# Two VectorE operations of a gate polynomial issued right behind the squares in every batch of a fused attention and expert kernel

## The chip, the cores and the metric

The kernel runs on one core of a Trainium2 chip. The metric is the device time of one launch in microseconds, as the median of several runs. Five engines work side by side, each through its own queue of instructions: TensorE (PE; its weight loads are shown as PEld), VectorE (DVE), ScalarE (ACT), GpSimd (POOL) and SyncE (SP), which here only issues DMAs.

## The reference

Attention with mixed heads, then a dense layer with an odd gate, then slots of experts. The part that the change touches is the second:

```python
x = attn_out.transpose(0, 2, 1, 3).reshape(B * S, H * D)   # 1792 tokens x 768
h = x @ w_in                     # w_in: 768 x 2048
g = h - np.tanh(h)
x = g @ w_out                    # w_out: 2048 x 768
# then: logits = x @ phi; softmax over tokens and over slots; experts; combine
```

## The kernel before, in words

The program is one sequence of Python calls under a manual schedule: each engine executes its instructions in the order in which the calls issue them, and semaphores are put in between by the framework.

After attention, stage 1 computes h and g in transposed form. The 1792 tokens are cut into four passes of 512, 512, 512 and 256 tokens, the 2048 features into 16 blocks of 128. A batch is one block of one pass, so there are 64 batches, numbered t. The function `step(t)` issues TensorE's product of batch t (18 matrix multiplies into one PSUM bank, tile `hp`, L830) and, through hooks between its six groups of three, everything else: the gate of batch t - 1, the transposition of the gate of batch t - 2 (`turn_g`, L900 on TensorE, copied out on ScalarE, L903), and side work.

The gate computes g = h - tanh(h), and for small h, where that difference would lose its digits, a polynomial in h squared. `gate_act` issues on ScalarE the square of h into the PSUM tile `sq` (L849), the square of the shifted square into `qd` (L850), tanh into `g` (L855) and a mask that is positive where h is small (`mk`, L856). Between the second square and tanh it calls `beside`, which splits the weights of batch t + 1 into a high and a low part, on ScalarE and GpSimd (L777 and L778 in pass 0, nothing in passes 1 and 2, halves at L786 and L787 towards pass 3). `gate_poly` issues two VectorE operations on `qd` and `sq` (L860, L861). `gate_first` subtracts tanh from h (L868), and `gate_last` finishes the polynomial into `hp` (L873) and copies it over `g` where the mask is set (L874). `gate_first` is issued at hook 1 and `gate_last` at hook 4. In pass 3 (`t >= LAST`, LAST = 48) `gate_act` itself calls `gate_poly`.

The side work of pass 0 (steps 3 to 16) prepares w_out @ phi: `turn_w` transposes three blocks of a weight at a time on TensorE (L953) into the PSUM bank that `turn_bank` hands out in turn (two banks, one used by `turn_g` in between), and a copy takes them out, on VectorE for the first half of a row of blocks (L959), on ScalarE for the second (L957). The first `turn_w` of a step is at hook 1 ahead of `gate_first`, the second at hook 3. The steps 5, 9, 13 and 16 also fold the transposed weights (L965, L973, L975). Steps 2 to 12 convert the last weights from 64-bit floats, on ScalarE (L50), VectorE (L54 to L66, five operations) and GpSimd (L71). In steps 8 to 13 the activations of the next pass are split, on ScalarE (L813) and GpSimd (L814). In steps 18 and 34 hook 1 begins with `mix_t` and `slot_exp`, whose first VectorE operation is a reduction (L1011).

Of the kernel before, what the change touches and what calls it, by code (L numbers as in the profile page):

```python
# [636 lines left out]
def moe_and_slots(tc, ident, xd, wi, wo, wo4, wis, consts, w1, w2, out, box):  # L637
# [27 lines left out]
    LAST = NST - NF  # L665
# [12 lines left out]
    def bank(tag, shape, name):  # L678
        return bank_pool[tag].tile(shape, FP32, tag=tag, name=name)
# [156 lines left out]
    def temps_of(t):  # L836
        n = PASS[t // NF]
        if t < 2:
            part = [quad[:, i * n:(i + 1) * n] for i in range(4)]
            return part[0], part[1], part[2], part[3] if t else mem["g0"]  # L840
        i = (t - LAST) % 2 * n if t >= LAST else 0
        return mem["sq"][t], mem["qd"][:, i:i + n], mem["mk"][:, :n], g_of(t)

    def gate_act(t, beside=None):
        hp = hps[t]
        if t > 1:
            mem["sq"] = {t: bank(f"q{t % 2}", [128, PASS[t // NF]], "sq")}
        sq, qd, mk, g = temps_of(t)
        nc.scalar.activation(out=sq, in_=hp, func=ACTF.Square)  # L849
        nc.scalar.activation(out=qd, in_=sq, func=ACTF.Square, bias=tshift)  # L850
        if t >= LAST:
            gate_poly(t)
        if beside:
            beside()
        nc.scalar.activation(out=g, in_=hp, func=ACTF.Tanh)  # L855
        nc.scalar.activation(out=mk, in_=sq, func=ACTF.Relu, bias=tlimit, scale=-1.0)  # L856

    def gate_poly(t):
        sq, qd, mk, g = temps_of(t)
        nc.vector.scalar_tensor_tensor(out=qd, in0=qd, scalar=TG_E, in1=sq, op0=ALU.add, op1=ALU.mult)  # L860
        nc.vector.scalar_tensor_tensor(out=qd, in0=sq, scalar=-TG_A, in1=qd, op0=ALU.add, op1=ALU.mult)  # L861

    def gate_first(t):
        hp = hps[t]
        sq, qd, mk, g = temps_of(t)
        if t < LAST:
            gate_poly(t)
        nc.vector.tensor_tensor(out=g, in0=hp, in1=g, op=ALU.subtract)  # L868

# [214 lines left out]
    def step(t):  # L1084
# [14 lines left out]
        if t > 2:  # L1099
            split_half(t + 1, 0)  # L1100
            gate_act(t - 1, lambda: split_half(t + 1, 1) if t >= NF else split_w(t + 1, nc.gpsimd))
        else:
            split_w(t + 1, nc.gpsimd)
# [4 lines left out]
        if t > 2:  # L1108
            on(1, gate_first, t - 1)
# [75 lines left out]
    load_w(4)  # L1185
    mem["g0"] = keep.tile([128, TM], FP32, tag="lp", name="g0")
    gate_act(0)
    yield
    split_w(2, nc.vector)
    product(1, {})  # L1190
    load_w(5)
    gate_first(0)
    gate_last(0)
    yield
    gate_act(1)
    while not box.get("go"):
        yield
    gate_first(1)
    gate_last(1)
    acc_stack = ExitStack()  # L1200
# [28 lines left out]
    t = NST  # L1229
# [300 lines left out]
```

## Time and profile before

| | us |
|---|---|
| median of three runs | 899.65 (894.24 to 904.73) |
| the profiled execution | 899.93 |
| its span | 898.2 |
| TensorE busy | 823.1 (92%) |
| ScalarE busy | 573.5 (64%) |
| VectorE busy | 556.1 (62%) |
| GpSimd busy | 257.0 (29%) |

The profile is of one execution. Stage 1 lies between 446 us and 790 us of its span: pass 0 up to about 556, passes 1 and 2 up to about 730, pass 3 up to about 787. In rows of the timeline the columns are start, length, engine, line, operation, output and inputs by name, shapes, and, in brackets, how long the engine was idle before and which instruction released it. The engines start an operation a little before the one ahead of it has ended, so the spacing of starts is the measure of a chain.

### The profile page before, as it was taken

Reading aid. Unit: us, or ns where it says so; the run is one execution under the profiler, and the core shown is the slowest. Engines: PE = TensorE matmul, PEld = TensorE weight load, DVE = VectorE, ACT = ScalarE, POOL = GpSimd, SP = SyncE. Lnnn points to the kernel's source line nnn. Section 1 sums busy time; section 2 is a strip of 40 time slices with the busy share of each in tenths; the row PEclk is TensorE's granted clock in tenths of the full one; section 3 lists DMA queues with packets and bytes.
Section 4 is the critical chain, followed back from the end, with each engine's and each line's share of the span. In section 5 each row is a group of like instructions: output and inputs, shape, how many; then the busy total and the mean of one; then the engine's idle time right before and its main releaser. Section 6 shows DMA issues by size and latency. Waiting matters only on the chain.

```text
span 898.2 us, 28617 instructions
## 1 busy us (share of the span) xinstructions
PE 823.1 (92%) x11760; PEld 581.5 (65%) x11760; DVE 556.1 (62%) x1181; ACT 573.5 (64%) x1351; POOL 257.0 (29%) x438
## 2 busy tenths in 40 slices
PE   8878989889987999999999899999999989999995
PEld 6456666666655666666776676767767767864542
DVE  4456857677766777777467886557776767720103
ACT  4766877778867788878656775647555656621013
POOL 6343434444434334434212561000000035500000
PEclk9989999999999999999999999999999999997998
DMA  6988889887989888774869976688745445899997
GB/s 133 227 215 231 220 215 235 238 226 215 226 217 236 233 208 243 238 216 154 261 216 374 346 243 215 258 306 325 284 162 176 158 141 193 284 380 426 416 372 267
DMA packets 145622, 222.95 MB, mean 248 GB/s; under 512 B 60820, under 2 KB 127444, under 8 KB 142036
## 3 DMA queue, kind: packets, MB, share of 16 engines
q1 hardware_dynamic: 142144, 208.26, 74.4%
q10 hardware_dynamic: 3348, 12.87, 3.6%
q8 instruction: 93, 1.52, 0.7%
q14 instruction: 37, 0.30, 0.1%
HBM read 146.39 MB, written 36.18 MB: 203 GB/s over the span
## 4 chain that ended last, share of the span: by engine, by line
PE 57%; ACT 13%; DMA 12%; DVE 12%; issue 4%; POOL 1%; SPq 0%; ACTq 0%; POOLq 0%; DVEq 0%
PE hp L830 21%; DMA D<-S 9%; PE pm L321 5%; ACT e L333 5%; PE vx L403 5%; PE sc L287 4%; PE tm L364 4%; DVE mx L325 3%; PE h L1314 3%; ACT S L295 2%; PE so L1355 2%; PE gt L900 2%; PE tz L1334 2%; ACT aT L378 2%; PE lgp L984 2%
## 5 line engine op out<-in xcount | busy, mean ns | idle before, releaser
L333 ACT ACTIVATE e<-pm,mx 128x448 f32<-128x448 f32 x184 | 115.1, 632 | 81.8 <-DVE mx L325 78.5
L830 PE MATMUL hp<-xa,rg 128*128 128x512 f32 x576 | 153.1, 405 | 0.6 <-ACT xa L813 0.4
L325 DVE TENSOR_REDUCE mx<-pm 128x1 f32<-128x448 f32 x184 | 106.1, 618 | 76.2 <-PE pm L321 76.0
L364 PEld LDWEIGHTS tm<-wk,e 64*56 64x56 f32 x5888 | 108.5, 130 | 57.0 <-issue 30.7
L321 PE MATMUL pm<-D,wpre 64*64 64x448 f32 (+2 forms) x736 | 113.0, 566 | 19.1 <-DMA D<-S 16.8
L364 PE MATMUL tm<-wk,e 64*56 64x60 f32 x5888 | 117.5, 218 | 10.1 <-issue 5.3
L830 PEld LDWEIGHTS hp<-xa,rg 128*128 128x128 f32 x576 | 102.2, 188 | 30.0 <-issue 10.5
L295 ACT ACTIVATE S<-sc 120x448 f32<-120x448 f32 (+1 forms) x186 | 91.4, 552 | 13.8 <-DMA kn<-in_k_dram 5.8
L287 PE MATMUL sc<-khi,qT 64*120 64x448 f32 (+1 forms) x384 | 84.0, 395 | 9.2 <-DVE xs L413 6.5
L787 POOL TENSOR_TENSOR rg<-rg 128x384 fp32r<-128x384 f32 x32 | 32.0, 1012 | 207.0 <-DVE rg L784 195.2
L339 POOL TENSOR_SCALAR rv<-ss 128x2 f32<-128x2 f32 x92 | 24.5, 267 | 229.1 <-ACT e L333 191.0
L350 POOL TENSOR_SCALAR wk<-wpost,rv 128x60 f32<-128x60 f32 x184 | 85.2, 494 | 16.2 <-DVE rv L343 14.5
L403 PE MATMUL vx<-aT,vn 128*64 128x120 f32 (+1 forms) x1536 | 85.3, 263 | 3.7 <-issue 3.2
L403 PEld LDWEIGHTS vx<-aT,vn 128*64 128x64 f32 x1536 | 74.8, 138 | 10.5 <-issue 5.6
L860 DVE SCALAR_TENSOR_TENSOR qd<-qd,sq 128x512 f32<-128x512 f32 (+1 forms) x62 | 38.3, 617 | 64.1 <-ACT mk L856 57.6
L849 ACT ACTIVATE sq<-hp 128x512 f32<-128x512 f32 (+1 forms) x62 | 32.8, 529 | 70.4 <-PE hp L830 70.2
L378 ACT ACTIVATE aT<-tm 128x480 f32<-128x480 f32 x144 | 75.8, 593 | 0.4 <-PE tm L364 0.4
L830 PE MATMUL hp<-xb,rg 128*128 128x512 f32 x288 | 74.7, 404 | 0.0
L287 PEld LDWEIGHTS sc<-khi,qT 64*120 64x120 f32 (+1 forms) x384 | 46.3, 176 | 26.1 <-PE tm L364 7.9
L830 PEld LDWEIGHTS hp<-xb,rg 128*128 128x128 f32 x288 | 52.0, 188 | 16.6 <-issue 6.3
L321 PEld LDWEIGHTS pm<-D,wpre 64*64 64x64 f32 (+2 forms) x736 | 24.8, 132 | 56.8 <-DMA D<-S 22.6
L71 POOL TENSOR_TENSOR fa<-fa,f 128x384 f32<-128x384 f32 x56 | 57.4, 1026 | 7.2 <-DVE rv L343 3.4
(194 smaller groups left out, 1407.9 us busy)
## 6 DMA issues: line engine op xcount, KB each, us to landing
ex<-in_moe_w_dram SPq DMA_DIRECT2D x25, 1536.0 KB
D<-S SPq DMA_DIRECT2D x144, 210.0 KB
rg<-wis SPq DMA_DIRECT2D x32, 768.0 KB
f<-in_moe_w_in_dram SPq DMA_DIRECT2D x32, 384.0 KB
wis<-rg ACTq DMA_DIRECT2D x16, 768.0 KB
rg<-wi SPq DMA_DIRECT2D x26, 384.0 KB
f<-in_moe_w_out_dram SPq DMA_DIRECT2D x24, 384.0 KB
wi<-fa SPq DMA_DIRECT2D x32, 192.0 KB
```

What stands on the lines that cost most here:

```text
L71: eng.tensor_tensor(out=out, in0=bits(a), in1=bits(p), op=ALU.add)
L287: nc.tensor.matmul(xs[e][0][:ni], lhsT=qT[n][s, l, p, :ni], rhs=kt[s], start=(i == 0), stop=(i == 2))
L295: nc.scalar.activation(out=dst, in_=xs[e][0][:ni], func=ACTF.Copy)
L321: nc.tensor.matmul(xs[x][64 * i:64 * i + 64], lhsT=wpre[k0:k1], rhs=d[i][k0:k1], start=True, stop=True)
L325: nc.vector.tensor_reduce(out=mx[:, x:x + 1], in_=xs[x], op=ALU.max, axis=AX.X, negate=True)
L333: nc.scalar.activation(out=es[x], in_=xs[x], func=ACTF.Exp, bias=mx[:, x:x + 1], accum_out=ss[:, x:x + 1])
L350: nc.gpsimd.tensor_scalar(out=wk, in0=wpost, scalar1=rv[:, x:x + 1], scalar2=None, op0=ALU.mult)
L364: nc.tensor.matmul(xs[i][64 * z:64 * z + JH, x, c], lhsT=es[x][h, j:j + JH], rhs=wks[x][h], start=True, stop=True)
L378: nc.scalar.activation(out=out[:, :, c0:c0 + m].rearrange("p a (x i) -> p a x i", x=2), in_=x, func=ACTF.Copy)
L403: nc.tensor.matmul(x[64 * e:64 * e + 64, i, :ni], lhsT=nat_v[b, h // NP][:, h % NP, c, :], rhs=a[:, c, h, :ni], start=(c == 0), stop=(c == ...
L830: nc.tensor.matmul(hp, lhsT=r32(w[:, m, hl, cs]), rhs=r32(x_of(b, c, l)), start=(c == 0 and i == 0), stop=(c == KD - 1 and i == 2))
L860: nc.vector.scalar_tensor_tensor(out=qd, in0=qd, scalar=TG_E, in1=sq, op0=ALU.add, op1=ALU.mult)
```

## The change

The two VectorE operations of `gate_poly` are issued by `gate_act` itself, right behind ScalarE's two squares, in the batches 2 to 47 as well as in pass 3; until now they were issued by `gate_first` in these. Batches 0 and 1 keep the old place. Nothing else is changed.

```diff
@@ gate_act
         nc.scalar.activation(out=sq, in_=hp, func=ACTF.Square)
         nc.scalar.activation(out=qd, in_=sq, func=ACTF.Square, bias=tshift)
-        if t >= LAST:
+        if t > 1:
             gate_poly(t)
         if beside:
             beside()
@@ gate_first
         sq, qd, mk, g = temps_of(t)
-        if t < LAST:
+        if t < 2:
             gate_poly(t)
         nc.vector.tensor_tensor(out=g, in0=hp, in1=g, op=ALU.subtract)
```

## Rows read from the trace of the kernel before

**Rows 1.** Busy time by stretch: PE, PEld, DVE, ACT, POOL, clock, DMA, GB/s

```profile
465.00:556.00 91.00, 85.45 (x470) 62.34 (x469) 70.08 (x125) 61.90 (x111) 38.86 (x27) 1.00 0.86 306
556.00:730.00 174.00, 173.44 (x884) 125.99 (x883) 116.92 (x196) 100.79 (x185) 2.03 (x2) 1.00 0.62 225
```

**Rows 2.** Waits of PE and of PEld from 465 to 730: total us, times, longest

```profile
PE wt L953 <- DVE ex L959: 3.2, 4, 1.1
...
PEld gt L900 <- issue: 3.5, 11, 0.5
```

**Rows 3.** Timeline of pass 1: the gate of one batch

```profile
600.62 0.58 ACT L849 ACTIVATE sq<-hp 128x512 f32<-128x512 f32 x1 [2.19 <-PE hp L830]
...
601.24 0.69 ACT L850 ACTIVATE qd<-sq,tshift 128x512 f32<-128x512 f32 x1
...
603.02 0.69 DVE L860 SCALAR_TENSOR_TENSOR qd<-qd,sq 128x512 f32<-128x512 f32 x1 [2.41 <-ACT mk L856]
603.74 0.69 DVE L861 SCALAR_TENSOR_TENSOR qd<-sq,qd 128x512 f32<-128x512 f32 x1
604.35 0.68 DVE L868 TENSOR_TENSOR g<-hp,g 128x512 f32<-128x512 f32 x1
...
605.67 0.75 DVE L874 COPY_PREDICATED g<-mk,hp 128x512 f32<-128x512 int32 x1
...
606.53 0.42 PEld L900 LDWEIGHTS gt<-ident,g 128*128 128x128 f32 x4 [0.36 <-issue]
```

**Rows 4.** Timeline of pass 3: squares, polynomial and mask of one batch

```profile
779.05 0.47 ACT L850 ACTIVATE qd<-sq,tshift 128x256 f32<-128x256 f32 x1
...
779.55 0.42 DVE L860 SCALAR_TENSOR_TENSOR qd<-qd,sq 128x256 f32<-128x256 f32 x1
...
780.01 0.43 DVE L861 SCALAR_TENSOR_TENSOR qd<-sq,qd 128x256 f32<-128x256 f32 x1
...
780.47 0.47 ACT L856 ACTIVATE mk<-sq,tlimit 128x256 f32<-128x256 f32 x1 [0.26 <-DVE qd L861]
```

**Rows 5.** Timeline of pass 0: steps 7 and 8, squares and second weight transposes

```profile
493.96 0.58 ACT L849 ACTIVATE sq<-hp 128x512 f32<-128x512 f32 x1 [1.16 <-PE hp L830]
...
496.61 0.49 PE L953 MATMUL wt<-ident,ex 128*128 128x128 f32 x3
...
499.21 0.58 ACT L849 ACTIVATE sq<-hp 128x512 f32<-128x512 f32 x1 [0.84 <-PE hp L830]
...
502.50 0.55 DVE L959 COPY ex<-wt 128x384 f32<-128x384 f32 x1
...
503.11 0.55 PE L953 MATMUL wt<-ident,ex 128*128 128x128 f32 x3 [1.10 <-DVE ex L959]
...
505.76 0.58 ACT L849 ACTIVATE sq<-hp 128x512 f32<-128x512 f32 x1 [0.62 <-PE hp L830]
```

**Rows 6.** L54 by line (ns min/median/max); timeline of one L54 beside GpSimd

```profile
L54 DVE TENSOR_SCALAR ex<-ex x8: 334/530/1440, 478.9 to 528.3; 128x384 f32<-128x384 f32 x8
...
521.30 1.29 POOL L814 TENSOR_TENSOR xb<-xb 128x512 fp32r<-128x512 f32 x1 [3.30 <-ACT xb L813]
521.37 1.44 DVE L54 TENSOR_SCALAR ex<-ex 128x384 f32<-128x384 f32 x1
```

**Rows 7.** Timeline of pass 0, step 15: mask, second weight transpose

```profile
551.21 0.69 ACT L856 ACTIVATE mk<-sq,tlimit 128x512 f32<-128x512 f32 x1
...
552.33 0.31 PEld L953 LDWEIGHTS wt<-ident,ex 128*128 128x128 f32 x3 [0.42 <-ACT ex L957]
```

**Rows 8.** Timeline at the entry into pass 3: gate transposes of batches 46 and 47

```profile
730.15 0.58 ACT L849 ACTIVATE sq<-hp 128x512 f32<-128x512 f32 x1 [1.28 <-PE hp L830]
...
731.93 0.63 PE L900 MATMUL gt<-ident,g 128*128 128x128 f32 x4 [1.10 <-ACT qd L850]
...
733.31 0.69 DVE L860 SCALAR_TENSOR_TENSOR qd<-qd,sq 128x512 f32<-128x512 f32 x1 [1.29 <-ACT mk L856]
...
736.84 0.63 PE L900 MATMUL gt<-ident,g 128*128 128x128 f32 x4 [2.15 <-DVE g L874]
```

## The prediction, made blind

> **What bounds the kernel now.** I first read the busy time of each engine over two stretches: the steps of stage 1 that also transpose and fold weights (465 to 556 us, pass 0) and the plain ones (556 to 730 us, passes 1 and 2) [rows 1]. The reader is to see that TensorE is busy for 173.44 of 174.00 us in the second and for 85.45 of 91.00 us in the first, at a granted clock of 1.00 in both. So nothing that VectorE does sooner can win more than 0.56 us plus what hides inside TensorE's rows in passes 1 and 2, or 5.55 us in pass 0. The change can cost any amount wherever TensorE waits for something that now comes later. The list of waits says where it waits today: above all, four times for VectorE's copy of a transposed weight, 3.2 us in all [rows 2].
>
> Then I read one batch of pass 1 in order of time [rows 3]. The squares start at 600.62, the second at 601.24 (0.69 long, so done at 601.93), but the polynomial starts only at 603.02, released by ScalarE's mask. It reads the same PSUM tile, sq, as the mask does. In pass 3, where the two operations already stand behind the squares, the order is the reverse [rows 4]: the polynomial starts at 779.55, 0.03 after the second square ends, and now the mask starts at 780.47, 0.03 after the polynomial ends, released by it. So whichever of the two readers of sq is issued first makes the other wait. The change doesn't take the wait away, it turns it round: the mask will wait for the polynomial in all 46 batches from 2 to 47.
>
> **What moves.** No instruction is added or removed, and the two operations issue no DMA. On VectorE they overtake the copy of a transposed weight (L959), where hook 1 begins with one, and in steps 18 and 34 the reduction of slot_exp; the SP and GpSimd queues are not overtaken, for the split of the weights puts work on ScalarE and GpSimd only. On ScalarE nothing is reordered, but the mask waits, and behind it stand the copies L903 and L957, the absolute value for the conversion, the activations split and the next squares. In steps 18 and 34 the reduction goes up to 1.33 later, but its result is transposed on TensorE only a step later, so I take 0. The store of split weights, a DMA that ScalarE's queue issues behind the mask in pass 0, is read again sixteen steps later: 0 as well.
>
> The new chain, from the spacing of starts in rows 3: polynomial at squares + 0.62 + 0.69 + 0.03 = 1.34 instead of 603.02 - 600.62 = 2.40; its second half 0.72 later, the next VectorE operation 0.61 after that, at 2.67. The second half ends at 2.75, so the mask goes to 2.79. The chain up to the predicated copy, which now ends at 605.67 + 0.75, 5.80 after the squares, gets 1.06 shorter, and more where a split copy stands between square and tanh.
>
> **Cost 1: the weight copy behind the polynomial (pass 0).** Steps 3 to 16 transpose weights. The PSUM banks of these transposes alternate, the gate's transpose taking the one in between, so the second weight transpose of a step needs the bank of the first to have been copied out. Where that copy is VectorE's (steps 3, 5 to 14 and 16, twelve of them) the polynomial is now ahead of it. In a step without a wait, TensorE begins the second weight transpose 496.61 - 493.96 = 2.65 after the squares, and the next squares come 499.21 - 496.61 = 2.60 later [rows 5]. With the change: copy at 2.67, transpose 503.11 - 502.50 = 0.61 later, at 3.28, and then 505.76 - 503.11 = 2.65 to the next squares. That is 3.28 + 2.65 - 5.25 = 0.68 us per step, all of it on TensorE. Steps 6, 10 and 14 follow a fold, whose last products and the logits stand on TensorE ahead of the product: squares and polynomial pass under them, so I take 0 (0.68 each without that cover). Steps 3, 5, 7, 13 and 16 pay in full: 5 x 0.68 = **3.4** (ends 0, if the polynomial slips ahead of the transpose unseen, and 5 x 1.33 = 6.7, if all of it shows).
>
> In steps 8, 9, 11 and 12 VectorE is behind with conversion work, and these are the waits that rows 2 count. Swapping two neighbours in a full queue delays the copy by the polynomial's 1.33 (0.72 + 0.61), but the chain behind it is shorter, and VectorE gets rid of its backlog sooner. If the copy then goes at the free pace, the four steps cost 4 x 0.68 - 3.2 = -0.5. What speaks against a full recovery is one row: a conversion operation that takes 334 ns at best took 1440 ns where it began 0.07 us after a GpSimd subtraction of 1.29 us had [rows 6]. With the conversion some 1.3 us earlier, it meets that subtraction more often. I take one such loss of 1.1 us among the four steps: -0.5 + 1.1 = **+0.6** (ends -0.5 and 4 x 1.33 = 5.3).
>
> **Cost 2: the mask behind the polynomial.** In steps 4 and 15 the first weight copy is ScalarE's, behind the mask, and TensorE already waits for it in step 15 [rows 7]. The mask there is 0.69 long, and with the polynomial right behind it, as in rows 3, it starts 2.40 - 0.69 - 0.03 = 1.68 after the squares. It will start at 2.79: 1.1 us. In step 4 a split copy stands between and hides most of this; I take 0.4. Sum **+1.5** (ends 0.4 and 2.2). In passes 1 and 2 the mask's 1.1 us falls into ScalarE's waits for the next product (2.19 us ahead of the squares in rows 3); if that cover were gone, each step could lose the rest, but 1.0 us of it is left.
>
> Pass 0 in sum: 3.4 + 0.6 + 1.5 = **+5.5 us**.
>
> **Gain 1: gate transposes (passes 1 and 2).** The predicated copy ended at 606.42, and TensorE's load for a gate transpose started at 606.53 after 0.36 us idle [rows 3]: the chain is a little late there. In the list of waits such idle times stand before eleven gate transposes, 3.5 us together [rows 2]; they are of the weight loads, so a part of each is hidden by the multiply in flight. A chain that is 1.06 shorter ends them: about 0.1 each, **-1.0** (ends 0 and -3.5).
>
> **Gain 2: entry into pass 3.** Batches of 256 tokens follow batches of 512, and the gates of batches 46 and 47 are late: TensorE waits 1.10 and 2.15 us at its gate transposes [rows 8]. The releaser named in one row is the next square; by the clock the predicated copy had just ended. The first chain is shortened by more than 1.10. For the second, the polynomial goes from 733.31 to 730.15 + 1.34 = 731.49, so its end comes 1.82 sooner; together the two transposes can come no sooner than that: **-1.8** (ends 0, if a later load takes it back, and -3.25).
>
> **Sum.** 5.5 - 1.0 - 1.8 = +2.7 us. The profiled execution took 899.93 us (span 898.2 and 1.7 around it) and the median is 899.65; the sum is made on the former and added to the latter: **902.3 us**. Three runs of one kernel already lie between 894.24 and 904.73, so 1% (9 us) is about what a measurement can tell from no change.
>
> **Rivals.** *Slower: GpSimd holds VectorE up.* If the conversion operations, earlier by about the polynomial, meet a GpSimd subtraction in all eight converting batches, each loses 1440 - 334 = 1.1 us [rows 6], which the copy behind them hands to TensorE: 8 x 1.1 = 8.8 in place of 0.6, a sum of 3.4 + 1.5 + 8.8 - 2.8 = +10.9, 910.5 us. It decides where the conversion ends later than 1.34 us after the squares. For it: VectorE is already full there. Against: the shortest of the eight took 334 ns and the median one 530, so today most of them pass with little. The Trainium skill (SBUF — State Buffer, "Who interferes with whom") states this as a rule: VectorE in a two-port mode and GpSimd exclude each other for the length of an instruction, and whoever issues first goes first; rows 6 agree. Chance 0.14.
>
> *Faster: the copies are hidden.* VectorE reaches the polynomial before TensorE's first weight transpose is done and the copy keeps its time; only the mask's 1.5 is left, and both gains come whole: 1.5 - 1.0 - 3.25 = -2.8, 896.9 us. Against it: the copy would have to start at 2.04 for a transpose at 2.65, and the polynomial isn't through until 2.67. Chance 0.2.
>
> *It doesn't do what it says.* If the polynomial still waited for ScalarE's newest instruction, nothing would move: 899.7 us. Rows 4 speak against it. Chance 0.05.
>
> **How the numbers follow.** The forecast has 0.58, and 0.03 is left for what I don't see. The range goes from 895 (the hidden copies, less a part of the spread of runs) to 910.5 (GpSimd in the way). Faster by over 1% needs both gains whole and a lucky run: 0.05. Slower by over 1% is most of the slower rival's chance and a little of the forecast's: 0.13. Within 1%: 0.82.
>
> **What would show it.** In the changed profile the polynomial is released by the second square, 1.34 after the first, and the mask by the polynomial. TensorE's wait for the copy L959 grows from four times to nine or so and from 3.2 us to some 6; a step like the seventh takes 5.9 instead of 5.25 us; the stretch up to the first products of pass 1 is about 5.5 us longer, passes 1 and 2 about 1 us shorter, and the two waits of 3.25 us at the entry into pass 3 shrink to about 1.4. I am wrong if the steps with conversion take much more or less than 6.2 us each, if TensorE waits for ScalarE in passes 1 and 2, or if the last part, which is the same in both, changes by more than these sums.

## The result and the profile after

The changed kernel takes 908.74 us (median of 20 runs, 900.95 to 916.99) where the kernel before, run beside it, takes 901.07 (20 runs, 894.24 to 912.87). The ratio is 1.0088 with a 95% interval of 1.0067 to 1.0110: 7.7 us slower, 0.9%. The forecast was +2.7 us. The time lies inside the range and within 1%, but the cost is almost three times the forecast. Medians here are over all runs, ratios over those that are not in the slower state (over 1.5% above the fastest run of their kernel), so a ratio can differ from that of the two medians.

The profiled execution of after took 904.51 us (span 902.8). Its mean granted clock is 0.985, where the median of its 20 runs is 0.978 and the profiled execution of before has 0.978: it had less time at the lower clock than a usual run. The two stretches of rows 1, from the same step to the same step (columns as there):

```profile
468.00:566.10 98.10, 86.57 (x470) 61.94 (x469) 73.42 (x125) 62.54 (x111) 38.99 (x27) 1.00 0.81 284
566.10:740.70 174.60, 172.63 (x885) 126.69 (x883) 118.05 (x198) 103.13 (x185) 2.03 (x2) 1.00 0.62 224
```

The first is 98.10 - 91.00 = 7.10 us longer, yet TensorE is busy only 86.57 - 85.45 = 1.12 us more in it: what was added is waiting, at a clock of 1.00. The second is 0.60 longer, and that is one step of pass 0 (step 16) that still lies in it.

The chain of the gate turned round as expected. Timeline of after, the batch of rows 3:

```profile
612.53 0.58 ACT L849 ACTIVATE sq<-hp 128x512 f32<-128x512 f32 x1 [1.86 <-PE hp L830]
...
613.14 0.69 ACT L850 ACTIVATE qd<-sq,tshift 128x512 f32<-128x512 f32 x1
...
613.87 0.69 DVE L860 SCALAR_TENSOR_TENSOR qd<-qd,sq 128x512 f32<-128x512 f32 x1 [2.35 <-ACT qd L850]
...
615.31 0.69 ACT L856 ACTIVATE mk<-sq,tlimit 128x512 f32<-128x512 f32 x1 [0.99 <-DVE qd L861]
...
616.58 0.74 DVE L874 COPY_PREDICATED g<-mk,hp 128x512 f32<-128x512 int32 x1
```

The polynomial starts 613.87 - 612.53 = 1.34 after the squares, released by the second square, and the mask 2.78 after them, released by the polynomial after 0.99 us of standing still. The predicated copy ends 4.79 after the squares (5.80 before).

The waits of TensorE from 468 to 741 (total us, times, longest), against rows 2:

```profile
PE wt L953 <- DVE ex L959: 8.3, 8, 3.5
...
PE wt L953 <- ACT ex L957: 2.2, 2, 1.1
...
PE sp L1066 <- ACT quad L903: 1.5, 1, 1.5
```

The wait for VectorE's weight copy grew from four times and 3.2 us to eight times and 8.3 us, and one of the eight is 3.5 us. Nothing in the forecast is that long. The wait at L1066, in passes 1 and 2, is another that the forecast doesn't have (0.4 before). The eleven short idle times at the gate's transposes [rows 2] have left the list.

To see where each microsecond went I took the length of every step, from the start of its first square (L849) to the start of the next step's, and subtracted the kernel before's. A step from 3 to 16 repeats to 0.03 us when the kernel before is run again, so these differences say more than whole runs do, which scatter by 5 us and more. All that differs by over 0.1 us in steps 3 to 16 (the later rows are explained with the experiments):

| us more than before, by step | 3 | 4 | 5 | 6 | 7 | 8 | 9 | 11 | 12 | 13 | 15 | 16 | pass 0 |
|---|---|---|---|---|---|---|---|---|---|---|---|---|---|
| after | .24 | .37 | .67 | -.31 | .68 | 1.37 | 1.07 | .59 | .67 | .69 | 1.11 | .65 | +7.8 |
| after_again | .22 | .38 | .66 | -.31 | .68 | 1.35 | 2.66 | .58 | .67 | .69 | 1.09 | .65 | +9.3 |
| pass0_only | .23 | .38 | .66 | -.32 | .68 | .44 | 2.84 | .59 | .65 | .69 | 1.11 | .66 | +8.6 |
| store_front | .24 | .39 | .66 | -.32 | .68 | -.60 | .66 | .59 | .67 | .69 | 1.10 | .66 | +5.4 |
| mask_first | .81 | .01 | 1.24 | -.31 | 1.26 | -.04 | .67 | .58 | .66 | 1.26 | .00 | 1.23 | +7.4 |
| hook4 | -.02 | -.31 | .04 | -.33 | .02 | 1.36 | 1.83 | -.68 | .58 | .38 | .41 | -.02 | +3.3 |
| combined | .01 | -.31 | .06 | -.32 | .03 | -.67 | .68 | -.69 | .59 | .37 | -.18 | -.02 | -.4 |

In after_again, pass0_only and hook4 step 9 holds a stretch at the lower clock, worth some 1.6 us (below). After's other parts: steps 18 to 48 (passes 1 and 2) -0.07, the step at the entry into pass 3 (step 49) -1.82, the steps behind it -1.10. The sum of the steps is +4.79.

Most steps are what was worked out: 0.65 to 0.69 where 0.68 was expected. Steps 8 and 9 are not. Timeline of after, steps 7 to 9:

```profile
497.93 0.58 ACT L849 ACTIVATE sq<-hp 128x512 f32<-128x512 f32 x1 [1.16 <-PE hp L830]
...
500.71 0.69 ACT L856 ACTIVATE mk<-sq,tlimit 128x512 f32<-128x512 f32 x1 [0.26 <-DVE qd L861]
...
500.77 0.33 ACTq L791 DMA_DIRECT2D wis<-rg  x1
...
503.86 0.58 ACT L849 ACTIVATE sq<-hp 128x512 f32<-128x512 f32 x1 [1.15 <-PE hp L830]
...
506.64 0.69 ACT L856 ACTIVATE mk<-sq,tlimit 128x512 f32<-128x512 f32 x1 [0.26 <-DVE qd L861]
...
508.08 0.52 SPq L766 DMA_DIRECT2D rg<-wi  x1
...
509.58 0.33 ACTq L791 DMA_DIRECT2D wis<-rg  x1
...
509.96 0.60 ACT L903 ACTIVATE quad<-gt 128x512 f32<-128x512 f32 x1 [2.63 <-PE hp L830]
...
510.82 0.55 ACT L50 ACTIVATE ex<-ex 128x384 f32<-128x384 f32 x1
...
511.40 0.36 DVE L54 TENSOR_SCALAR ex<-ex 128x384 f32<-128x384 f32 x1 [2.28 <-ACT ex L50]
...
511.97 1.34 POOL L814 TENSOR_TENSOR xb<-xb 128x512 fp32r<-128x512 f32 x1 [3.80 <-ACT xb L813]
...
512.19 1.53 DVE L60 SCALAR_TENSOR_TENSOR ex<-ex 128x384 int32<-128x384 int32 x1
...
516.43 0.55 PE L953 MATMUL wt<-ident,ex 128*128 128x128 f32 x3 [3.45 <-DVE ex L959]
```

Follow ScalarE's queue. The store of split weights (L791) left at 500.77, 2.84 after the squares and 0.06 after the held mask began; in before it left at 494.64, 0.68 after the squares of the same step, while split, tanh and mask, which stand ahead of it in the program, had yet to begin. In the next step the mask starts at 506.64, and then ScalarE does nothing until its store gets away at 509.58: the 2.63 us of idle time at L903 (the releaser printed there, a product of TensorE, had long been done). Behind the store stand the copy L903 and the absolute value L50 of the weight conversion. VectorE idles 2.28 us for that value, the conversion's next operation L60 then falls on a GpSimd subtraction (1.53 us instead of 0.56), VectorE's weight copy comes late, and TensorE waits 3.45 us for it in step 9. Before, the store of step 8 left at 501.31, 2.10 after its squares; after, 5.72 after them.

### The profile page after: what moved, and what is told of

Same layout as the page of the kernel before. It is cut to its first block, busy times and chain, and to the rows that moved or that the text cites. A ratio compares the mean times of both kernels' runs of the same rounds, so it can differ in the third digit from the quotient of the medians.

```text
span 902.8 us, 28655 instructions
## 1 busy us (share of the span) xinstructions
PE 818.9 (91%) x11760; PEld 580.1 (64%) x11760; DVE 559.4 (62%) x1181; ACT 576.5 (64%) x1351; POOL 257.0 (28%) x438
## 3 DMA queue, kind: packets, MB, share of 16 engines
q8 instruction: 93, 1.52, 0.7%
## 4 chain that ended last, share of the span: by engine, by line
PE 55%; DMA 16%; ACT 12%; DVE 10%; issue 4%; POOL 1%; ACTq 0%; SPq 0%; POOLq 0%; DVEq 0%
PE hp L830 20%; DMA D<-S 7%; PE pm L321 6%; PE vx L403 5%; ACT e L333 5%; PE sc L287 5%; DMA ex<-in_moe_w_dram 5%; PE tm L364 4%; DVE mx L325 3%; ACT S L295 2%; PE gt L900 2%; DMA ex<-wo 2%; ACT aT L378 2%; PE sp L1066 1%; PE h L1314 1%
## 5 line engine op out<-in xcount | busy, mean ns | idle before, releaser
L364 PE MATMUL tm<-wk,e 64*56 64x60 f32 x5888 | 116.8, 217 | 14.9 <-issue 10.8
L856 ACT ACTIVATE mk<-sq,tlimit 128x512 f32<-128x512 f32 (+1 forms) x62 | 39.2, 632 | 43.3 <-DVE qd L861 43.3
L849 ACT ACTIVATE sq<-hp 128x512 f32<-128x512 f32 (+1 forms) x62 | 32.9, 530 | 45.5 <-PE hp L830 45.0
```

The lines of the kernel that those rows point to most:

```text
L364: nc.tensor.matmul(xs[i][64 * z:64 * z + JH, x, c], lhsT=es[x][h, j:j + JH], rhs=wks[x][h], start=True, stop=True)
```

## The experiments

Three theories were weighed. *Order*: VectorE's copy stands behind the polynomial on its own queue, and each step pays for that, whatever else goes on. *Store*: the store behind the held mask comes late, and what waits for it holds up step 8 or 9. *Full VectorE*: conversion and polynomial together are too much for VectorE in the full steps, or GpSimd holds it up; this is the slower rival grown large.

**Half of the change each.** In one kernel the early polynomial is kept in passes 1 and 2 alone, in another in pass 0 alone:

```
late_only:   gate_act: if t >= NF: gate_poly(t)                     gate_first: if t < NF: ...
pass0_only:  gate_act: if 1 < t < NF or t >= LAST: gate_poly(t)     gate_first: if t < 2 or NF <= t < LAST: ...
```

> Only the batches from 16 on (steps 17 to 48) have the polynomial early; the batches 2 to 15 are as before. If pass 0 pays and the later passes gain (my theory): ratio to before 0.997 to 0.999 (about -1.5 us for gate transposes, -1.8 at the entry into pass 3, +1.1 at the first sum over slots in step 22). If the mask's wait costs ScalarE something in every later step, the ratio is 1.003 or more. Pass 0 should take the same time as in the kernel before, within 0.5 us.

> Only the batches 2 to 15 (steps 3 to 16) have the polynomial early. If pass 0 pays: 6 to 8 us from the squares of step 3 to those of step 19 over the kernel before, and a ratio of 1.006 to 1.009. If the loss lies in the later passes, the ratio is below 1.003.

late_only: 894.95 against 902.22 us, ratio 0.9923 [0.9890, 0.9957], below the 0.997 to 0.999 that were expected. pass0_only: 909.02 against 902.22, ratio 1.0079 [1.0043, 1.0115]. So the loss is all in pass 0, and the rest of the change is a gain. By the steps, late_only has +0.16 up to the end of pass 0, the -1.82 of the entry and after's +1.1 in step 20 (the expectation calls it step 22); pass0_only has after's pass 0 but for steps 8 and 9, and none of these. In pass0_only ScalarE's idle time behind the store in step 8 is 1.68 us, and what it delays shows in step 9 (timeline of pass0_only):

```profile
510.91 0.33 ACTq L791 DMA_DIRECT2D wis<-rg  x1
...
511.29 0.60 ACT L903 ACTIVATE quad<-gt 128x512 f32<-128x512 f32 x1 [1.68 <-DMA ex<-wo]
```

**The same kernels again**, to see what is scatter (no edit).

> The changed kernel once more. If ScalarE's idle 2.6 us in step 8, between the mask and the next DMA issue, belongs to the change, it is there again, and steps 8 and 9 again cost 2.4 us more than before; if it was chance, steps 8 and 9 cost 0.5 us or less each and pass 0 as a whole some 5.5 us.

> The kernel before once more. It shows how far the same stretches differ from run to run: the first profiled runs of the two kernels differ by 3.0 us ahead of step 3, and by 3 us the other way in the experts' part, where the code is the same; I expect differences of that size here, and the steps of passes 0 to 2 the same within 0.3 us.

after_again: 910.33 us, pass 0 +9.3, with 2.66 in step 9 instead of 1.07 and the other steps from 3 to 16 within 0.03. Step 9 in after and in after_again (stretches, columns as in rows 1):

```profile
511.78:521.15 9.37, 5.92 (x34) 3.17 (x33) 9.04 (x15) 5.62 (x12) 5.41 (x4) 1.00 0.81 282
```

```profile
515.26:526.22 10.96, 7.52 (x34) 3.47 (x33) 9.37 (x15) 5.60 (x11) 6.41 (x5) 0.84 0.89 293
```

TensorE is busy for 7.52 - 5.92 = 1.60 us more with the same 34 entries, at a mean granted clock of 0.84 instead of 1.00, and the step is 1.59 longer: the difference between the two runs is the clock. In after_again the clock fell behind TensorE's wait of 3.44 us for the weight copy; in after, behind a wait of 3.45, it stayed. Step 9 has such a stretch in pass0_only (0.85) and in hook4 (0.83) too, behind waits of 2.90 and 2.52 us. So of pass0_only's 2.84 some 1.6 are the clock, and its steps 8 and 9 cost less than after's at equal clock: ScalarE's idle time there is 1.68 us instead of 2.63.

before_again: 908.32 us. Its steps 2 to 48 repeat within 0.04 us; it starts step 1 at 463.99 us, 10.8 later than the first profile of the same kernel, its entry into pass 3 is 1.5 longer, and later steps of pass 3 give 1.5 back. The entry in before and in before_again:

```profile
734.01:740.12 6.11, 3.96 (x32) 2.81 (x31) 4.99 (x11) 3.09 (x8) 2.89 (x4) 1.00 0.74 247
```

```profile
744.84:752.44 7.60, 5.48 (x32) 3.48 (x31) 4.97 (x11) 3.08 (x8) 3.00 (x4) 0.78 0.58 200
```

Here too the 1.5 us are the clock: 0.78 instead of 1.00, with TensorE busy for 1.52 us more.

**The store ahead of the mask.** After, with the store issued in front of the split and the tanh of the same step:

```
 def beside():
     if t >= NF: split_half(t + 1, 1)
+    else: save_w(t); split_w(t + 1, nc.gpsimd)
-if b == 0: on(1, save_w, t)
+if t == 2: on(1, save_w, t)
```

> The changed kernel, with the store of the split weights (L791, on ScalarE's queue) issued behind the second square, ahead of tanh and the mask, where it left the queue before the change. If the held mask delays the store, and through it SyncE's next loads and the next store's own wait: ScalarE's idle 1.7 to 2.9 us in steps 8 and 9 is gone, these two steps cost 0.7 us or less each over the kernel before, and pass 0 costs about 5.5 us instead of 7.8 to 9.3. If the idle time belongs to the place in the program or to GpSimd's lock, it stays and pass 0 costs the same.

The long wait is gone; all steps but 8 and 9 keep after's length. Timeline of store_front, steps 7 and 8, and its waits of TensorE:

```profile
498.32 0.58 ACT L849 ACTIVATE sq<-hp 128x512 f32<-128x512 f32 x1 [1.16 <-PE hp L830]
...
499.00 0.33 ACTq L791 DMA_DIRECT2D wis<-rg  x1
...
504.93 0.33 ACTq L791 DMA_DIRECT2D wis<-rg  x1
...
507.04 0.69 ACT L856 ACTIVATE mk<-sq,tlimit 128x512 f32<-128x512 f32 x1 [0.26 <-DVE qd L861]
...
507.62 0.59 ACT L903 ACTIVATE quad<-gt 128x512 f32<-128x512 f32 x1
```

```profile
PE wt L953 <- DVE ex L959: 6.3, 8, 1.5
```

The store leaves 499.00 - 498.32 = 0.68 after the squares, as in before, and L903 follows the mask without idle time. Steps 8, 9, 11 and 12 together: +1.3 us instead of after's +3.7. Step 8 is now 0.60 shorter than before: it pays its 0.68 and gets back a wait. Timed: 905.25 against 900.67 us, ratio 0.9985 [0.9940, 1.0031].

SyncE shows who else waits for the store: its load of the next raw weights (L766) into the buffer that the store reads from. Its waits from 465 to 575 (total, times, longest), in before, after and store_front in this order:

```profile
SPq L766 <- DMA wis<-rg: 32.5, 10, 6.8
```

```profile
SPq L766 <- DMA wis<-rg: 47.8, 8, 8.8
```

```profile
SPq L766 <- DMA wis<-rg: 27.7, 8, 6.6
```

**The weight copy out of the polynomial's way.** After, with the second weight transpose one hook later, `on(4, turn_w, *ws[1])` for `on(3, ...)`, so that VectorE's copy has the polynomial's time to spare:

> The changed kernel, with the second weight transpose of a step asked for one group of three multiplies (0.94 us) later. If TensorE waits because the bank's copy stands behind the polynomial (ready 3.28 us after the squares, wanted at 2.65): the 0.68 us of steps 5, 7, 13 and 16 goes to 0.1 or less, and so does TensorE's wait for L959 there. If the steps are longer for another reason (VectorE's load, the mask), they stay longer by 0.6 us.

Timeline of hook4, step 7:

```profile
492.46 0.58 ACT L849 ACTIVATE sq<-hp 128x512 f32<-128x512 f32 x1 [0.88 <-PE hp L830]
...
495.13 0.55 DVE L959 COPY ex<-wt 128x384 f32<-128x384 f32 x1
...
495.81 0.49 PE L953 MATMUL wt<-ident,ex 128*128 128x128 f32 x3
...
497.73 0.58 ACT L849 ACTIVATE sq<-hp 128x512 f32<-128x512 f32 x1 [0.49 <-PE hp L830]
```

The copy starts 2.67 after the squares, as worked out, the transpose, one hook later, starts at 3.35 without waiting, and the step takes 5.27 us, 0.02 more than in before. The 0.68 is gone from steps 3, 5, 7 and 16, and step 8 still costs 1.36: the two costs are separate. (Of the 1.83 in step 9 some 1.6 are the clock.) Timed: 901.69 against 900.67 us, ratio 0.9991 [0.9947, 1.0034].

**The same edit in the kernel before** asks how much of this hook4 would have won anyway.

> The kernel before with only the second weight transpose one group later. If that transpose waits for the bank's copy in four full steps there (3.2 us), these waits shrink by up to 0.94 us each and pass 0 gets up to 3 us shorter; if VectorE itself sets the pace of these steps, they stay within 0.3 us.

905.1 us in a single run. Its full steps 8, 9, 11 and 12 are 1.8 us shorter than before's together. Its steps 3 to 16 are +0.3 us all the same, for step 10 is 2.4 longer. There the granted clock fell for some 3 us (stretches of hook4_before, columns as in rows 1):

```profile
522.00:525.00 3.00, 3.00 (x15) 2.02 (x8) 0.16 (x1) 1.18 (x2) 2.11 (x2) 0.56 1.01 307
```

The rest of the 2.4 is in the main a longer wait of TensorE for the fold's copy L975 (1.26 us, 0.38 in before). If a stretch at the lower clock is put at 1.6 us, as measured in step 9 of after_again, pass 0 without it is 0.3 - 1.6 = -1.3 in hook4_before and 3.3 - 1.6 = +1.7 in hook4. By this estimate the hook is worth some 1.3 us by itself, and of the 6.1 us that hook4 wins over after in pass 0 (7.8 - 1.7) some 4.8 are cost of the change.

**The conversion left out.** Before and after, without the five VectorE operations of the last weights' conversion (`on(5, late_first, t - 4)` and `f64_tail` removed), so that VectorE is not full; the values of the last output weights are then not computed.

> The kernel before without the five VectorE operations of the conversion in steps 4 to 12 (L54 to L66 for the last weights are left out, the rest stays). It is the base for the next run: the waits of TensorE for L959 in steps 8, 9, 11 and 12 (3.2 us) should be gone.

> The changed kernel without the same five operations. If a full VectorE makes steps 8, 9, 11 and 12 dear, they cost the free 0.68 us each against the run above. If the delayed store does it, ScalarE's idle time ahead of its DMA issue stays in steps 8 and 9 and they cost 2 us or more together over 1.4.

Between these two, the early polynomial costs 0.67, 1.29, 0.68 and 0.66 us in steps 8, 9, 11 and 12, and 7.7 over pass 0: as much as with the conversion. The waits of TensorE in noconv_after:

```profile
PE wt L952 <- DVE ex L958: 3.7, 8, 0.5
```

Eight waits of at most 0.5 us, with no conversion to be late; ScalarE still idles 1.6 us at L903, and that shows in step 9 alone, as 0.6 more than the free price. Against noconv_before, the conversion in before costs 1.29 + 0.99 + 0.74 + 1.02 = 4.04 us in these four steps; in after, against noconv_after, 4.04 + 3.70 - 3.30 = 4.44. So a loss of this size doesn't need a full VectorE: the free price alone, 0.67 four times, is most of it. With the conversion there is a wait to win back, and the late store, which holds the conversion's first operation on ScalarE, takes it again. That rules out the third theory as the main cause; it doesn't show that GpSimd took no part (see below, on the full steps without the store).

**The mask ahead of the polynomial.** After, but for the batches from 2 to 47 the mask is issued right behind the squares, so that ScalarE isn't held and VectorE is, for the mask's length:

```
+    early = 1 < t < LAST
+    if early: nc.scalar.activation(out=mk, in_=sq, func=ACTF.Relu, bias=tlimit, scale=-1.0)
     if t > 1: gate_poly(t)
     ...
-    nc.scalar.activation(out=mk, ...)
+    if not early: nc.scalar.activation(out=mk, ...)
```

> The changed kernel with the mask issued right behind the squares in batches 2 to 47, ahead of polynomial, split and tanh, so that ScalarE isn't held and the polynomial waits 0.58 us for the mask. If the held mask makes the losses of steps 15 and 20 and the idle time ahead of the store in steps 8 and 9, these go to 0.1 us or less; and if the order on VectorE makes that of steps 5, 7, 13 and 16, it grows from 0.68 to about 1.25 us each. If the polynomial's place as such makes the loss in 15 and 20, they stay.

Timeline of mask_first, step 7 (lines 953 and 959 are 957 and 963 here):

```profile
499.14 0.58 ACT L849 ACTIVATE sq<-hp 128x512 f32<-128x512 f32 x1 [1.16 <-PE hp L830]
...
499.82 0.33 ACTq L791 DMA_DIRECT2D wis<-rg  x1
...
502.38 0.55 DVE L963 COPY ex<-wt 128x384 f32<-128x384 f32 x1
...
502.99 0.55 PE L957 MATMUL wt<-ident,ex 128*128 128x128 f32 x3 [1.03 <-DVE ex L963]
```

The copy starts 3.24 after the squares instead of 2.67, and steps 5, 7, 13 and 16 cost 1.23 to 1.26 each. The store leaves 0.68 after the squares again. What came from the held ScalarE is gone: steps 4 and 15 cost 0.01 and 0.00, step 20 costs 0.00, step 8 is 0.04 shorter than before and step 9 costs the 0.67 of any other. The whole took 906.72 us in a single run, pass 0 +7.4. This shows a second time, with the store's place in the program untouched, that steps 8 and 9 were dear because of ScalarE.

**All remedies together.** The early polynomial except in batches 14, 18, 19 and 34 (where a held mask shows), the store in front, and the later hook; beside it late_only once more.

> The changed kernel with the store in front of tanh (as in store_front), the second weight transpose one group later (as in hook4), and the old place of the polynomial in the four batches 14, 18, 19 and 34, where something on TensorE waits for a copy of ScalarE behind the mask (steps 15, 19, 20 and 35). If the three costs are what I take them for: pass 0 1 to 2 us shorter than in the kernel before, passes 1 and 2 1.4 us shorter, the entry into pass 3 1.8 us shorter, so a ratio of about 0.995. If the costs trade places, pass 0 is no shorter than before and the ratio is 0.997 or more.

> The kernel with the early polynomial from batch 16 on once more, timed again. Its steps were 2.3 us shorter than before, its median 7 us. If only the steps count, the ratio is 0.996 to 0.999 now; if something outside of stage 1 changes with it, the ratio is again 0.993 or less.

combined: 897.06 against 904.07 us, ratio 0.9941 [0.9897, 0.9985], its steps 4.4 us shorter than before's: faster than the kernel before, and so than after. TensorE's waits for the copy are back at before's size (of combined):

```profile
PE wt L953 <- DVE ex L959: 3.2, 3, 1.4
```

late_again: 897.59 against 904.07, ratio 0.9946 [0.9911, 0.9981], between the two expectations, so it doesn't decide between them. Of combined's 4.4 us pass 0 gives only 0.4 where 1 to 2 were expected, less than the 1.3 estimated for the hook alone: in pass 0 the early polynomial buys nothing even with its costs removed. Passes 1 and 2 give 1.1 (1.4 expected). The kernel that follows from this, the early polynomial in passes 1 and 2 alone except in the batches where the mask shows, with the later hook, was not run.

## Why the prediction was right or wrong

**Right: the mechanism and most prices.** The polynomial 1.34 after the squares, the mask at 2.78 (2.79 predicted). Free steps 3, 5, 7, 13 and 16: 2.93 us for a predicted 3.4, four of them 0.65 to 0.69 each and step 3 only 0.24. hook4 shows the cause: with the transpose out of the copy's way they cost at most 0.04, but for step 13 (0.38; the hook alone costs 0.56 there in hook4_before). Step 6, taken as 0, gained 0.31. Steps 4 and 15: 1.48 for 1.5. The entry into pass 3: -1.82 for -1.8. Its two waits, 1.10 and 2.15 us in rows 8, in after:

```profile
741.41 0.60 PE L900 MATMUL gt<-ident,g 128*128 128x128 f32 x4
...
745.73 0.66 PE L900 MATMUL gt<-ident,g 128*128 128x128 f32 x4 [1.57 <-DVE g L874]
```

The first has no wait left, the second 1.57 us (1.4 predicted for both). This step takes 4.29 to 4.31 us in the eight profiles that have after's order in batches 46 and 47. With the old order there it took 6.11 in the first profile of before and 7.60 to 7.64 in the four others (before_again, pass0_only, noconv_before, hook4_before). The clock is the difference: 0.78 over this step in these four, where it fell behind TensorE's wait of over 2 us, and 1.00 in before's first profile and in the eight. So the term is -1.8 at equal clock, and against four of five profiles with the old order 1.5 more. That the shorter waits are what keeps the clock up in the eight fits this count; no run shows it by itself.

**Wrong: the store taken as "0 as well".** The prediction counted the moved DMA by who reads its result, sixteen steps later. It didn't ask who waits for the buffer that it empties, and what stands behind it on the queue that issues it. The full steps 8, 9, 11 and 12 cost 3.7 us where +0.6 was predicted; with the store in front they cost 1.3. So 2.4 us are the store's, and in after_again 1.6 more, the clock that fell behind the long wait. Steps 8 and 9 take 7.92 and 9.37 us, a sign of being wrong that the prediction named (6.2 for each; step 9 took 8.30 already in before).

**Mis-sized: the full steps without the store.** The 1.3 that are left are 0.7 more than the +0.6: only step 8 gets its wait back (-0.60), where the prediction let all four go at the free pace. It took one more loss of 1.1 us to GpSimd; there were more. By line (ns min/median/max) of after:

```profile
L54 DVE TENSOR_SCALAR ex<-ex x8: 339/354/361, 481.6 to 534.7; 128x384 f32<-128x384 f32 x8
...
L55 DVE TENSOR_SCALAR ex<-ex x8: 360/361/1337, 482.0 to 535.1; 128x384 int32<-128x384 int32 x8
...
L60 DVE SCALAR_TENSOR_TENSOR ex<-ex x8: 557/560/1534, 482.4 to 536.5; 128x384 int32<-128x384 int32 x8
...
L65 DVE TENSOR_SCALAR ex<-ex x8: 348/355/1307, 488.5 to 541.7; 128x384 int32<-128x384 int32 x8
```

Five of the forty operations are held, each by 0.96 to 0.98 us while a subtraction L814 of 1.28 to 1.34 us runs on GpSimd: L60 at 512.19 and 528.61, L55 at 518.70 and 535.13, L65 at 541.65. Before, one was held by 1.1 and four by about 0.4. So the meeting that the slower rival asked for did happen, in four of its eight batches (in one of them twice), and VectorE lost 4.9 us to it instead of 2.6. Steps 9, 11 and 12, which don't get their wait back, are steps whose weight copy stands behind a held operation; in step 8 none was held. No run moves GpSimd's subtraction alone, so its share of the 1.3 us is argued, not shown; and though the timing lies nearer to the rival's 910.5 us than to the forecast, it wasn't reached by the rival's mechanism, whose 8.8 us here are not there. The Trainium skill states, beside the rule cited with that rival (SBUF — State Buffer, "Who interferes with whom"), that a VectorE instruction with two inputs in SBUF contends with a GpSimd instruction that reads SBUF. L60 has two, and the trace agrees: 1.53 us beside a subtraction of 1.34.

What the late store hits first in step 8 stays open. SyncE's load behind it goes 508.08 - 503.86 = 4.22 after the squares, 3.18 in before (502.39). ScalarE's store of the same step waits until 509.58, and the trace names no releaser for it. (For the longest such idle time it names a transfer in pass0_only and in noconv_after, but not the same one: `ex<-wo` and `rg<-wi`.) That the store's place is the cause is shown by store_front and, from the other side, mask_first; which transfer was the last to hold L791 isn't.

**Wrong: the mask's hold in passes 1 and 2 taken as hidden.** It mostly is, but the prediction said what it would cost if the cover were gone and then didn't look for the steps without cover. A wait of TensorE for ScalarE in these passes was one of its signs of being wrong, and it came. The dear step is step 20. Timeline of after:

```profile
591.78 0.58 ACT L849 ACTIVATE sq<-hp 128x512 f32<-128x512 f32 x1 [0.98 <-PE hp L830]
...
594.56 0.69 ACT L856 ACTIVATE mk<-sq,tlimit 128x512 f32<-128x512 f32 x1 [0.99 <-DVE qd L861]
595.15 0.59 ACT L903 ACTIVATE quad<-gt 128x512 f32<-128x512 f32 x1
...
595.79 0.62 PE L1066 MATMUL sp<-quad,es 128*32 128x512 f32 x2 [1.52 <-ACT quad L903]
```

The slot sums want the block that ScalarE copies right behind the mask, so the 1.1 us show on TensorE (its wait was 0.42 in before): +1.11. mask_first and combined, which don't hold the mask there, have 0.00 and 0.01 in step 20. Two other pairs of steps, 18 and 19 (-0.21, +0.19) and 34 and 35 (-0.14, +0.15), cancel; combined keeps them though the mask isn't held in 19 and 35, so they are not the mask's. The remaining steps gained 1.2 for a predicted 1.0 at the gate transposes, so passes 1 and 2 come out at nothing.

**Sum.** Pass 0 +7.8, passes 1 and 2 about 0, the entry -1.8: +5.9 us where 5.5 - 1.0 - 1.8 = +2.7 was predicted. The difference of 3.2 is the store (2.4), the rest of the full steps (0.7) and the mask's hold in step 20 (1.1), less some smaller gains. In after_again 1.6 us of lower clock come on top, +7.5. Behind the entry the profiled execution gives 1.1 back: its step 58 is 1.4 shorter than before's, which waited for transfers there, and in before_again, the same code as before, that step is 1.0 shorter too. So this can't be put down to the change, and with it the steps add up to +4.8 and +6.3. The timing gives +7.7 with an interval of 6.0 to 9.9 (901.07 times the bounds of the ratio).

**Still open.** By the steps after's profile is less dear than its timing. A part may be the clock: the profile had 0.985 and no lower stretch in stage 1, a usual run 0.978. late_only's steps are 2.3 us shorter than before's, and its medians 7.3 and 6.5 us lower (intervals of the two ratios: 3.9 to 9.9 us, 1.7 to 8.0). Here the mean granted clock of its runs is 0.981 both times, that of the runs of before beside them 0.978 and 0.977; 0.003 to 0.004 of 900 us is some 3 us, an estimate of what that gives. Why the clock differs isn't shown. store_front's steps are 4.0 longer; its median is 4.6 higher, its ratio leaves anything from -5.4 to +2.8 us. The two halves of the change, timed alone, add up to about nothing (6.8 - 7.3), where the whole costs 7.7; by the steps they give +9.5 and -2.3 (some 3 of the 9.5 are lower clock in steps 9 and 49), the whole +4.8 and +6.3. The parts ahead of stage 1 and behind it run the same code in all kernels, but the one ahead takes from 452.2 to 464.0 us in the profiles and the one behind from 108.2 to 111.6, so these can't place the rest.

## What to carry to other kernels

An instruction that is made to wait takes its whole queue with it, DMA issues included: list what stands behind it, and for each DMA ask both who reads what it writes and who waits to overwrite what it reads. When two engines read one PSUM tile one after the other, issuing one sooner only chooses who waits; here that paid where VectorE was the late one (passes 1 and 2, entry into pass 3) and cost where its other work or ScalarE's was wanted first. Steps that repeat to hundredths of a microsecond let an edit be read to a tenth, where whole runs scatter by 1%; but look at the granted clock of each step first, for one stretch at the lower level added 1.5 to 1.6 us to a step here, whatever the edit had done to it.

## What the runs showed of the hardware that was not expected

In step 7 of before, ScalarE's queue issued its store 0.68 us after the squares although three compute instructions that stand ahead of it in the program had yet to begin (in steps 8 and 9 it went 2.10 and 2.25 after them); in step 7 of after, with a mask among them that had to wait, it went 2.84 after the squares. In the next step the compute work behind the store began only when the store had gone, 2.63 us late.

Steps 3 to 48 of the kernel before repeat to 0.04 us between its two profiles, while the attention part ahead of them, the same code in all kernels, started step 1 anywhere from 452.2 to 464.0 us.

Stretches of some three to seven microseconds at the lower clock level appear amid the work of every profile from stage 1 on. In stage 1 they came where TensorE had just waited: in step 9 behind waits of 3.44, 2.90 and 2.52 us for L959 (after_again, pass0_only, hook4), in step 10 behind one of 1.26 us (hook4_before), and in the four long entries into pass 3, with TensorE busy for 0.88 of the 3.00 us ahead in before_again. Yet after's wait of 3.45 us in step 9 wasn't followed by one. The first profile of before has this one behind stage 1 (stretches of before):

```profile
809.00:815.00 6.00, 5.45 (x25) 1.03 (x25) 1.23 (x6) 0.68 (x2) 0.00 (x1) 0.54 1.01 430
```

A clock of 0.54 to 0.56 is mostly the lower of the two levels (1.2 GHz). This one began within 806 to 809 us, and from 803 to 806 TensorE had been busy for 3.00 of 3.00 us at a clock of 1.00. So waits stand ahead of many of these stretches, but the rows show no common cause.
